# Moving two coefficient broadcasts behind the second half's loads at the start of an attention and two-network kernel

## The chip, the cores and the metric

One Trainium2 chip, of which the kernel uses one core. The metric is the device time of one execution in microseconds (us), as the median of several runs; less is better.

The engines are named as the profile names them: PE does the matmuls, DVE and ACT the elementwise work, POOL a part of it, and SP issues the transfers (DMAs). An engine takes its instructions strictly in the order in which the built program lists them, so an instruction that waits holds up everything behind it on its engine.

## The reference

Three stages follow each other: a linear attention with a decaying state, over 4 batches, 8 heads, 768 steps and head size 48; a network with a rational activation (384 to 2048 to 384); and a network with a softmax-like activation and a normalisation (384 to 1024 to 384), both over 3072 tokens.

```python
for t in range(S):                       # attention
    state = alpha[:, :, t, :, None] * state + np.einsum('bhd,bhe->bhde', k[:, :, t], v[:, :, t])
    y[:, :, t] = np.einsum('bhd,bhde->bhe', q[:, :, t], state)
...
h = x @ w_in                             # first network
P = a[0] + a[1] * h + a[2] * h2 + a[3] * h3
Q = 1.0 + np.abs(b[0]) * np.abs(h) + np.abs(b[1]) * h2
x = (P / (Q + 1e-06)) @ w_out
...
h = x @ w_in                             # second network
e = np.exp(h - h_max)
solu = h * e / (e.sum() + 1e-09)
out = ((solu - mu) / np.sqrt(var + 1e-06) * g_ln) @ w_out
```

The change concerns `a` (4 numbers) and `b` (2 numbers), the coefficients of the rational function.

## The kernel before

The 768 steps are cut into 6 chunks of 128 steps. A chunk of attention is done in two halves of two batches each, so that there are halves 0 to 11. The first network runs over 6 chunks of 16 blocks (`m_up` and `m_down`), while the halves of the chunks ahead are worked in between; the second network follows. The weights arrive as raw 64-bit data: `split_w` loads a tile (L533), makes a 32-bit float of it by three DVE instructions (L537, L540, L541), rounds it on ACT (L547) and takes the rest on POOL (L548).

The start of the program is the function `network(True)` from L806 on. Half 0 loads `alpha`, `k` and `q` (`a_load(0)`, L266, four transfers each), one weight tile, and `v` (`v_load(0)`, L348, two transfers). Then stands `consts()`: two small transfers that copy `a` and `b` into all 128 partitions (L113 into `ab`, L114 into `bb`), four tiny ACT instructions (L115, L117 to L119), a memset (L125) and 19 tiny DVE instructions (L120 to L139) that work out the coefficients `co`. Their first user is the first block of the first network (L599). After `consts()` come one more weight tile, `a_load(1)` and `v_load(1)` for half 1. PE transposes what half 0 and half 1 loaded (L363), DVE runs the decays over it (the scans of L374 and L378, the end values of L375 and L376, the products of L382 and L383), and `a_pe` does the matmuls of a half (L420, L444, L483) with an evacuation on ACT (L427) and on ACT and DVE (L470, L471).

The order on the engines is not the order of the source: the framework's scheduler lists each engine's instructions by a simulated timeline, in which the source order decides among what is ready. All these transfers go through SP's queue. The framework gives SP's transfers eight semaphores in turn, so that a transfer is issued only when the one eight places ahead of it has landed.

Names in the rows: `lent` is one of two borrowed buffers, of which one takes half 1's `alpha`, `k` and `q` (printed as `lent_128`) and the other a weight tile and half 1's `v` (`lent_175` before, `lent_149` after the change; the number is only a counter). `st` is the other place for a raw weight tile, `vns` half 0's `v`, `tp` a transposed tile, `qks` and `kns` half 0's operands.

Of the kernel before, what the change touches and what calls it, by code (L numbers as in the profile page):

```python
# [19 lines left out]
def _view(ap, off, dims):  # L20
    return bass.AP(ap.tensor, ap.offset + off, [list(ap.ap[0])] + [list(d) for d in dims])


def _run(*gens):
    for g in gens:
        for _ in g:
            pass
# [3 lines left out]
def kernel(  # L31
# [78 lines left out]
    def consts():  # L110


        nc.sync.dma_start(out=ab, in_=bass.AP(moe_a.tensor, moe_a.offset, [[0, 128], [1, 4]]))  # L113
        nc.sync.dma_start(out=bb, in_=bass.AP(moe_b.tensor, moe_b.offset, [[0, 128], [1, 2]]))  # L114
        nc.scalar.activation(babs, bb, AF.Abs)  # L115
        cf, lin, rc, beta, rest, t, base = (co[:, 2 * x:2 * x + 2] for x in range(7))
        nc.scalar.activation(cf[:, 0:1], bb[:, 1:2], AF.Abs)  # L117
        nc.scalar.activation(cf[:, 1:2], ab[:, 3:4], AF.Abs)
        nc.scalar.activation(lin[:, 0:1], bb[:, 0:1], AF.Abs)  # L119
        nc.vector.tensor_scalar(sign, ab[:, 3:4], 0.0, 2.0, ALU.is_ge, ALU.mult)  # L120
        nc.vector.tensor_scalar(sign, sign, 1.0, None, ALU.subtract)
        nc.vector.tensor_tensor(lin[:, 1:2], ab[:, 2:3], sign, ALU.mult)
        nc.vector.tensor_tensor(base[:, 1:2], ab[:, 1:2], sign, ALU.mult)
        nc.vector.tensor_tensor(a0s, ab[:, 0:1], sign, ALU.mult)
        nc.vector.memset(base[:, 0:1], QC)  # L125
        nc.vector.tensor_scalar(bad[:, 4 * NCH:4 * NCH + 2], cf, C_MIN, None, ALU.is_lt)
        nc.vector.tensor_scalar(cf, cf, C_MIN, None, ALU.max)
        nc.vector.reciprocal(rc, cf)
        nc.vector.scalar_tensor_tensor(beta, lin, 0.5, rc, ALU.mult, ALU.mult)
        nc.vector.tensor_tensor(t, beta, beta, ALU.mult)  # L130
        nc.vector.tensor_tensor(t, t, cf, ALU.mult)
        nc.vector.tensor_scalar(bad[:, 4 * NCH + 2:], t, BETA * BETA, None, ALU.is_gt)
        nc.vector.tensor_scalar(beta, beta, B_MAX, -B_MAX, ALU.min, ALU.max)
        nc.vector.tensor_tensor(t, beta, beta, ALU.mult)
        nc.vector.tensor_tensor(base, base, rc, ALU.mult)
        nc.vector.tensor_tensor(rest, base, t, ALU.subtract)
        nc.vector.tensor_tensor(a0s, a0s, rc[:, 1:2], ALU.mult)
        nc.vector.tensor_tensor(back, cf[:, 1:2], rc[:, 0:1], ALU.mult)
        nc.vector.tensor_tensor(back, back, sign, ALU.mult)  # L139
# [13 lines left out]
    def network(fast):  # L153
# [30 lines left out]
        def clear():  # L184
            nc.gpsimd.memset(d1, 0.0)
            nc.gpsimd.memset(_view(d1[:], 0, [[PER, NB6 + 1]]), 1.0)
            nc.gpsimd.memset(d2, 0.0)
            nc.vector.memset(alT[:, 0:1], 0.0)
# [3 lines left out]
        def borrow(n, o, dims):  # L192
            if n not in lent:
                lent[n] = moe_pool.tile([128, GW], F32, name=f"lent{n}", tag=f"g{n}")
            size = 1
            for d in dims:
                size *= d
            t = lent[n][:, o:o + size]
            if len(dims) == 1:
                return t  # L200
            nm = "abcd"[:len(dims)]
            return t.rearrange(f"p ({' '.join(nm)}) -> p {' '.join(nm)}", **dict(zip(nm, dims)))
# [44 lines left out]
        def slot(i, x):  # L247

            c, bp = divmod(i, 2)
            return c, 2 * bp + x // 2, 4 * (x % 2)  # L250

        def a_load(i, names=("ra", "rk", "rq")):
            for x, (src, nm) in enumerate(((alpha, "ra"), (k, "rk"), (q, "rq"))):
                if nm not in names:
                    continue
                if i == 1:
                    t = borrow(3, 2048 + 1024 * x, [16 * D + 16])
                elif i == 0 and nm == "rq":
                    t = borrow(3, 5120, [16 * D + 16])
                else:  # L260
                    t = ap_.tile([128, 16 * D + 16], F32, name=nm, tag="rk" if nm == "rk" else "ra")
                if i < NPE:
                    nc.gpsimd.memset(t[:, 16 * D:], 1.0)
                for y in range(B):
                    c, b, h = slot(i, y)
                    nc.sync.dma_start(  # L266
                        out=t[32 * y:32 * y + 32, :16 * D].rearrange("p (h x) -> p h x", h=4),
                        in_=src[b, h:h + 4, CH * c:CH * c + CH, :].rearrange("h (j r) d -> j h (r d)", r=4),
                    )
                raws[i, nm] = t  # L270
                yield

        def a_move_qk(i):
            qk, kb = moved[i]
            for m, i0, n, d0 in ((0, 0, 32, 0), (1, 0, 16, 32), (1, 16, 16, 64), (2, 0, 32, 80)):
                nc.sync.dma_start(out=qks[d0:d0 + n], in_=qk[m].rearrange("b i x -> i b x")[i0:i0 + n])
            yield
# [64 lines left out]
        def v_load(i):  # L342
            vn = vts[i] = borrow(2, 1024, [B * 256]) if i == 1 else vns
            if i < NPE:
                nc.vector.memset(_view(vn[:], D, [[64, 4 * B], [1, 16]]), 0.0)
            for x in range(2):
                c, b, h = slot(i, 2 * x)
                nc.sync.dma_start(  # L348
                    out=vn[:, 512 * x:512 * x + 512].rearrange("p (h d) -> p h d", h=H)[:, :, :D],
                    in_=v[b, :, CH * c:CH * c + CH, :].rearrange("h t d -> t h d"),  # L350
                )
# [48 lines left out]
        def a_prep(i):  # L400
            if i >= NPE:
                yield from a_dve(i)

        def a_enter(i):
            if i < NPE:
                v_load(i)
                yield from a_turn(i)
            else:
                yield from a_move(i)
# [142 lines left out]
        def w1_group(n):  # L552
            w = moe_pool.tile([128, GW], F32R, name=f"g{n}", tag=f"g{n}")
            hi, lo = (w[:, 512 * KT * x:512 * KT * (x + 1)].rearrange("p (a b) -> p a b", a=KT) for x in range(2))
            for kt in range(KT):
                split_w(moe_w_in[128 * kt:128 * kt + 128, 512 * n:512 * n + 512], hi[:, kt, :], lo[:, kt, :])
                yield
            wi[n] = (hi, lo)
            hi, lo = (w[:, 4 * DM * x:4 * DM * (x + 1)].rearrange("p (a b) -> p a b", a=4) for x in range(2, 4))
            for f in range(4):  # L560
                r0 = 512 * n + 128 * f
                split_w(moe_w_out[r0:r0 + 128, :], hi[:, f, :], lo[:, f, :])
                yield
            wo[n] = (hi, lo)
# [9 lines left out]
        def x_load(c):  # L574
            for kt in range(KT):
                nc.sync.dma_start(
                    out=x_tile(c)[:, kt].rearrange("p a t -> p (a t)").bitcast(F32), in_=y_d[c][128 * kt:128 * kt + 128, :]
                )
# [217 lines left out]
        def take(g, n):  # L796
            for _ in range(n):
                if next(g, "end") == "end":
                    return False
            return True  # L800
# [5 lines left out]
        if fast:  # L806
            stage["wide"] = True
            stage["bank"] = "x2"
            pre = w1_group(0)
            _run(a_load(0))  # L810
            take(pre, PRE[0])
            v_load(0)
            consts()
            take(pre, PRE[1])
            _run(a_load(1))
            take(pre, PRE[2])
            v_load(1)
            take(pre, PRE[3])
            nc.gpsimd.memset(Sbd, 0.0)
            _run(a_turn(0), a_pe(0), a_turn(1), a_pe(1), pre)  # L820
            clear()
            pre = w1_group(1)
            take(pre, NA)
            _run(a_load(2, ("ra", "rk")))
            with tc.issue_after(marks[0, 1].ins):
                _run(a_prep(2))
            _run(a_move_qk(2))
            _run(a_enter(2), pre)
            _run(a_load(3, ("ra", "rk")))
            stage["wide"] = False  # L830
            stage["near"] = True
            stage["bank"] = "at"
        else:
            for n in range(NG):
                _run(w1_group(n))
            x_load(0)
# [190 lines left out]
    with tc.If(wide > 0):  # L1027
        recurrence()
        network(False)
# [30 lines left out]
```

## Time and profile before

| | |
|---|---|
| median of 3 runs | 778.04 us (775.98 to 781.6) |
| the profiled execution's own time | 776.87 us |
| its span in the profile | 775.0 us |
| PE busy | 728.0 us (94% of the span) |
| DVE busy | 630.4 us (81%) |
| ACT busy | 535.2 us (69%) |
| POOL busy | 358.4 us (46%) |

The profiled execution's own time is 1.9 us more than its span. It lies 1.2 us under the median. Each share is an average over the whole span; the stretches below have different limits. In a row of the timeline the first number is the start and the second the length in us from the span's start, and the bracket gives the idle time of that engine just before and what ended it.

### The profile page before, as it was taken

Reading aid. Unit: us, or ns where it says so; the run is one execution under the profiler, and the core shown is the slowest. Engines: PE = TensorE matmul, PEld = TensorE weight load, DVE = VectorE, ACT = ScalarE, POOL = GpSimd, SP = SyncE. Lnnn points to the kernel's source line nnn. Section 1 sums busy time; section 2 is a strip of 40 time slices with the busy share of each in tenths; the row PEclk is TensorE's granted clock in tenths of the full one; section 3 lists DMA queues with packets and bytes.
Section 4 is the critical chain, followed back from the end, with each engine's and each line's share of the span. In section 5 each row is a group of like instructions: output and inputs, shape, how many; then the busy total and the mean of one; then the engine's idle time right before and its main releaser. Section 6 shows DMA issues by size and latency. Waiting matters only on the chain.

```text
span 775.0 us, 13914 instructions
## 1 busy us (share of the span) xinstructions
PE 728.0 (94%) x4976; PEld 605.8 (78%) x4976; DVE 630.4 (81%) x1110; ACT 535.2 (69%) x983; POOL 358.4 (46%) x306
## 2 busy tenths in 40 slices
PE   4676999999999999999999999999999999999996
PEld 3565767788888787778877788888888989988986
DVE  4999999989898989899898966478887788877640
ACT  2245867689878888788878887788965545555541
POOL 3255777777554355434444433332243343452322
PEclk9857899999999999999999999999999999999999
DMA  7995446466837382727554350720025253542653
GB/s 167 253 275 165 107 155 167 146 147 206 204 99 161 122 205 83 172 66 207 137 148 91 124 82 1 296 112 0 1 83 132 89 130 90 132 108 52 140 119 76
DMA packets 87278, 101.74 MB, mean 131 GB/s; under 512 B 34464, under 2 KB 63136, under 8 KB 87200
## 3 DMA queue, kind: packets, MB, share of 16 engines
q1 hardware_dynamic: 87104, 100.67, 48.9%
q8 instruction: 41, 0.67, 0.4%
q14 instruction: 37, 0.30, 0.1%
q10 hardware_dynamic: 96, 0.10, 0.0%
HBM read 60.59 MB, written 27.56 MB: 114 GB/s over the span
## 4 chain that ended last, share of the span: by engine, by line
DVE 30%; PE 18%; ACT 12%; issue 5%; SPq 3%; DMA 3%; POOL 1%; ACTq 0%; DVEq 0%; POOLq 0%
PE x2p L638 6%; PE hp L592 6%; DVE room L752 3%; SPq L762 3%; DVE room L735 2%; DVE p L618 2%; ACT jk L737 2%; PE op L776 2%; DVE hp L622 2%; DVE w L621 2%; DMA room<-room 2%; DVE sm L731 2%; DVE room L750 2%; PE h L712 2%; DVE p L623 2%
## 5 line engine op out<-in xcount | busy, mean ns | idle before, releaser
L592 PE MATMUL hp<-xt,g 128*128 128x512 f32 x864 | 224.1, 401 | 14.8 <-DVE p L616 7.5
L626 POOL TENSOR_TENSOR gl<-p,gh 128x512 fp32r<-128x512 f32 x96 | 130.8, 1362 | 193.9 <-ACT gh L625 107.9
L592 PEld LDWEIGHTS hp<-xt,g 128*128 128x128 f32 x864 | 163.2, 192 | 54.2 <-DVE p L616 7.7
L638 PE MATMUL x2p<-gh,g 128*128 128x512 f32 x576 | 196.9, 395 | 2.0 <-ACT x2e L646 2.0
L638 PEld LDWEIGHTS x2p<-gh,g 128*128 128x128 f32 x576 | 107.9, 188 | 29.1 <-ACT x2e L646 4.7
L638 PE MATMUL x2p<-gl,g 128*128 128x512 f32 x288 | 112.9, 392 | 0.0
L776 PE MATMUL op<-w2oh,room 128*128 128x384 f32 x384 | 101.8, 339 | 1.3 <-ACT room L767 0.7
L768 POOL TENSOR_TENSOR room<-room,room 128x1024 fp32r<-128x1024 f32 x22 | 54.8, 2496 | 101.0 <-ACT room L767 79.0
L621 DVE SCALAR_TENSOR_TENSOR w<-w,co,hp 128x512 f32<-128x512 f32 x84 | 62.0, 738 | 43.5 <-ACT hp L620 42.5
L712 PE MATMUL h<-w2ih,x 128*128 128x512 f32 x288 | 90.7, 394 | 0.0
L599 ACT ACTIVATE p<-hp,co 128x512 f32<-128x512 f32 x96 | 66.0, 687 | 12.3 <-POOL gl L626 12.0
L620 ACT ACTIVATE hp<-ah 128x512 f32<-128x512 f32 x84 | 50.1, 597 | 33.3 <-DVE p L618 32.0
L776 PEld LDWEIGHTS op<-w2oh,room 128*128 128x128 f32 x384 | 70.1, 188 | 3.0 <-ACT room L767 1.0
L600 ACT ACTIVATE w<-ah,co 128x512 f32<-128x512 f32 x96 | 69.4, 724 | 1.7 <-DVE hp L622 1.3
L618 DVE SCALAR_TENSOR_TENSOR p<-p,co,hp 128x512 f32<-128x512 f32 x84 | 61.6, 734 | 9.3 <-ACT p L599 9.0
L597 ACT ACTIVATE ah<-hp 128x512 f32<-128x512 f32 x96 | 56.7, 591 | 16.4 <-PE hp L592 16.0
L776 PE MATMUL op<-w2ol,room 128*128 128x384 f32 x192 | 65.0, 339 | 0.0
L625 ACT ACTIVATE gh<-p 128x512 fp32r<-128x512 f32 x96 | 59.9, 623 | 5.7 <-DVE p L623 2.8
L638 PEld LDWEIGHTS x2p<-gl,g 128*128 128x128 f32 x288 | 54.1, 188 | 11.7 <-issue 0.8
L712 PEld LDWEIGHTS h<-w2ih,x 128*128 128x128 f32 x288 | 53.9, 188 | 11.7
L623 DVE SCALAR_TENSOR_TENSOR p<-p,co,hp 128x512 f32<-128x512 f32 x84 | 61.9, 737 | 1.1
L619 ACT ACTIVATE ah<-w,co 128x512 f32<-128x512 f32 x84 | 60.6, 721 | 1.3
(168 smaller groups left out, 1264.7 us busy)
## 6 DMA issues: line engine op xcount, KB each, us to landing
room<-room SPq DMA_DIRECT2D x96, 128.0 KB, 2.3
qk_d<-qk SPq DMA_DIRECT2D x10, 771.0 KB, 4.1
st<-in_moe_w_in_dram SPq DMA_DIRECT2D x13, 512.0 KB, 4.6
st<-in_moe_w_out_dram SPq DMA_DIRECT2D x16, 384.0 KB, 3.5
qks<-qk_d SPq DMA_DIRECT2D x20, 257.0 KB, 4.4
x<-x_d SPq DMA_DIRECT2D x18, 256.0 KB, 3.1
out_dram<-o SPq DMA_DIRECT2D x94, 48.0 KB, 1.6
ra<-in_alpha_dram SPq DMA_DIRECT2D x44, 96.0 KB, 2.8
```

Of the source, the lines that this page charges most:

```text
L592: last["PE", u] = nc.tensor.matmul(hp, lhsT=w[:, kt, 128 * o:128 * o + 128], rhs=xts[c][:, kt, xx, :], start=(kt == 0 and w is hi and xx = ...
L599: nc.scalar.activation(p, hp, AF.Square, bias=co[:, 7:8])
L600: nc.scalar.activation(w, ah, AF.Square, bias=co[:, 6:7])
L618: nc.vector.scalar_tensor_tensor(p, p, a1, hp, ALU.add, ALU.mult)
L619: nc.scalar.activation(ah, w, AF.Ln, bias=rest)
L621: nc.vector.scalar_tensor_tensor(w, w, rest, hp, ALU.add, ALU.mult)
L623: fin[u] = nc.vector.scalar_tensor_tensor(p, p, a0, hp, ALU.add, ALU.mult)
L625: last["ACT", u] = nc.scalar.activation(gh, p, AF.Copy)
L626: last["POOL", u] = nc.gpsimd.tensor_tensor(gl, p, gh[:].bitcast(F32), ALU.subtract)
L638: nc.tensor.matmul(x2ps[c][d], lhsT=w[:, o, 128 * d:128 * d + 128], rhs=gg, start=(f == 0 and w is hi and gg is gh), stop=(f == NF1 - 1 an ...
L712: nc.tensor.matmul(hp[:, 512 * n:512 * n + 512], lhsT=x2s[c][:, kt, x, CH * b:CH * b + CH], rhs=w2[w][:, kt, 512 * n:512 * n + 512], start ...
L776: nc.tensor.matmul(op, lhsT=x[:, 128 * f:128 * f + 128], rhs=w2[w][:, f, :], start=(f == 0 and x is hi and w == "oh"), stop=(f == NF2 - 1 ...
```

## The change

The call of `consts()` moves from behind `v_load(0)` to behind `v_load(1)`. Nothing else in the source changes.

```diff
             v_load(0)
-            consts()
             take(pre, PRE[1])
             _run(a_load(1))
             take(pre, PRE[2])
             v_load(1)
+            consts()
             take(pre, PRE[3])
```

On SP, behind the load of half 0's `v`, the built program before has:

```order
L348 DMA vns<-in_v_dram 128x8x48 x2
L113 DMA ab<-in_moe_a_dram 128x4
L114 DMA bb<-in_moe_b_dram 128x2
L533 DMA lent_175<-in_moe_w_in_dram 128x512
L266 DMA lent_128<-in_alpha_dram 32x4x192 x4
L266 DMA lent_128<-in_k_dram 32x4x192 x4
L266 DMA lent_128<-in_q_dram 32x4x192 x4
L348 DMA lent_175<-in_v_dram 128x8x48 x2
L533 DMA st<-in_moe_w_in_dram 128x512
```

and after the change:

```order
L348 DMA vns<-in_v_dram 128x8x48 x2
L533 DMA lent_149<-in_moe_w_in_dram 128x512
L266 DMA lent_128<-in_alpha_dram 32x4x192 x4
L266 DMA lent_128<-in_k_dram 32x4x192 x4
L266 DMA lent_128<-in_q_dram 32x4x192 x4
L348 DMA lent_149<-in_v_dram 128x8x48 x2
L113 DMA ab<-in_moe_a_dram 128x4
L114 DMA bb<-in_moe_b_dram 128x2
L533 DMA st<-in_moe_w_in_dram 128x512
```

The two broadcasts moved past one weight tile and 14 loads of half 1; the weight tile into `st` is next behind them now.

On DVE, behind the second scan of half 0 (L374), before:

```order
L540 SCALAR_TENSOR_TENSOR fp<-st,fp 128x512
L120 TENSOR_SCALAR co<-ab 128x1
L375 TENSOR_SCALAR qks<-Pp 128x4
L126 TENSOR_SCALAR bad<-co 128x2
L541 SCALAR_TENSOR_TENSOR ft<-st,fp 128x512
L121 TENSOR_SCALAR co<-co 128x1
L376 RECIPROCAL Rp<-qks 128x4
L127 TENSOR_SCALAR co<-co 128x2
L383 TENSOR_TENSOR qks<-tp,Pp 128x4x128
L537 TENSOR_SCALAR fp<-lent_175 128x512
```

and after, from the same place:

```order
L540 SCALAR_TENSOR_TENSOR fp<-st,fp 128x512
L375 TENSOR_SCALAR qks<-Pp 128x4
L541 SCALAR_TENSOR_TENSOR ft<-st,fp 128x512
L376 RECIPROCAL Rp<-qks 128x4
L383 TENSOR_TENSOR qks<-tp,Pp 128x4x128
L537 TENSOR_SCALAR fp<-lent_149 128x512
L378 SCALAR_TENSOR_TENSOR Rp<-tp,Rp,zero 128x127 x4
L540 SCALAR_TENSOR_TENSOR fp<-lent_149,fp 128x512
L382 TENSOR_TENSOR qks<-tp,Rp 128x4x128
L374 SCALAR_TENSOR_TENSOR Pp<-tp,zero 128x128 x4
L541 SCALAR_TENSOR_TENSOR ft<-lent_149,fp 128x512
```

The reader of `ab` (L120) and the first reader of what ACT makes of `bb` (L126) no longer stand in front of L541. They stand further down now, inside half 1's first pair of head groups, among the scans of L378:

```order
L375 TENSOR_SCALAR end_392<-Pp 128x4
L376 RECIPROCAL Rp<-end_392 128x4
L378 SCALAR_TENSOR_TENSOR Rp<-tp,Rp,zero 128x127 x3
L120 TENSOR_SCALAR co<-ab 128x1
L378 SCALAR_TENSOR_TENSOR Rp<-tp,Rp,zero 128x127
L121 TENSOR_SCALAR co<-co 128x1
L126 TENSOR_SCALAR bad<-co 128x2
L382 TENSOR_TENSOR lent_128<-tp,Rp 128x4x128
```

Beyond that the scheduler gave other orders on all engines up to the end of the first network's first chunk (about 185 us in the trace); behind that the lists of the path that runs are equal.

## Rows read from the trace of the kernel before

**Rows 1.** Stretches: length, busy time (count) of each engine, granted clock, DMA share, GB/s.
```profile
13.00:20.00 7.00, 1.15 (x18) 0.96 (x16) 3.32 (x14) 2.48 (x9) 2.63 (x4) 0.85 0.79 173
20.00:60.00 40.00, 29.46 (x323) 24.76 (x323) 39.07 (x95) 13.98 (x30) 15.51 (x16) 0.71 0.95 263
60.00:150.00 90.00, 77.94 (x542) 61.33 (x546) 88.65 (x148) 64.74 (x118) 68.65 (x58) 0.91 0.52 144
150.00:185.00 35.00, 35.00 (x248) 28.53 (x240) 31.58 (x51) 29.69 (x55) 24.82 (x22) 1.00 0.60 155
```

**Rows 2.** Timeline of DVE, 13 to 30 us.
```profile
13.25 0.67 DVE L540 SCALAR_TENSOR_TENSOR fp<-st,fp 128x512 int32<-128x512 int32 x1
...
16.02 0.17 DVE L126 TENSOR_SCALAR bad<-co 128x2 f32<-128x2 f32 x1 [1.97 <-ACT co L117]
...
16.89 0.68 DVE L383 TENSOR_TENSOR qks<-tp,Pp 128x512 f32<-128x512 f32 x1
19.29 0.69 DVE L537 TENSOR_SCALAR fp<-lent 128x512 int32<-128x512 int32 x1 [1.71 <-DMA lent<-in_moe_w_in_dram]
...
20.17 1.58 DVE L378 TENSOR_TENSOR_SCAN Rp<-tp,Rp,zero 128x127 f32<-128x127 f32 x4
...
22.32 0.15 DVE L135 TENSOR_TENSOR co<-co 128x2 f32<-128x2 f32 x1
22.39 0.15 DVE L137 TENSOR_TENSOR co<-co 128x1 f32<-128x1 f32 x1
...
29.49 0.67 DVE L383 TENSOR_TENSOR lent<-tp,Pp 128x512 f32<-128x512 f32 x1
```

**Rows 3.** Timeline of SP's issues, 6 to 23 us.
```profile
6.92 1.06 SPq L348 DMA_DIRECT2D vns<-in_v_dram  x2
8.03 2.82 SPq L113 DMA_DIRECT2D ab<-in_moe_a_dram  x1
10.88 0.43 SPq L114 DMA_DIRECT2D bb<-in_moe_b_dram  x1
11.36 0.44 SPq L533 DMA_DIRECT2D lent<-in_moe_w_in_dram  x1
11.84 1.85 SPq L266 DMA_DIRECT2D lent<-in_alpha_dram  x4
13.74 5.85 SPq L266 DMA_DIRECT2D lent<-in_k_dram  x4
...
21.53 1.16 SPq L348 DMA_DIRECT2D lent<-in_v_dram  x2
22.74 0.65 SPq L533 DMA_DIRECT2D st<-in_moe_w_in_dram  x1
```

**Rows 4.** Half microseconds of the same view as rows 1.
```profile
12.00:12.50 0.50, 0.50 (x14) 0.50 (x12) 0.50 (x3) 0.00 (x0) 0.00 (x0) 1.00 0.18 20
...
13.00:13.50 0.50, 0.50 (x10) 0.50 (x10) 0.50 (x3) 0.20 (x1) 0.00 (x0) 1.00 0.03 1
13.50:14.00 0.50, 0.50 (x12) 0.46 (x10) 0.50 (x3) 0.00 (x0) 0.00 (x0) 1.00 0.75 91
```

**Rows 5.** DMA issues of 8 to 12 us: count, KB each, us to landing.
```profile
lent<-in_moe_w_in_dram SPq DMA_DIRECT2D x1, 512.0 KB, 7.9
...
ab<-in_moe_a_dram SPq DMA_DIRECT2D x1, 2.0 KB, 5.0
bb<-in_moe_b_dram SPq DMA_DIRECT2D x1, 1.0 KB, 4.8
```

**Rows 6.** DMA issues of 22 to 23 us, the second of half 1's v loads among them.
```profile
st<-in_moe_w_in_dram SPq DMA_DIRECT2D x1, 512.0 KB, 5.3
lent<-in_v_dram SPq DMA_DIRECT2D x1, 192.0 KB, 4.0
```

**Rows 7.** SP's issue behind two v loads later in the kernel.
```profile
159.30 2.96 SPq L282 DMA_DIRECT2D kns<-kb_d  x1
```

**Rows 8.** Longest wait of DVE from 60 to 185 us: total, times, longest.
```profile
DVE hp L610 <- ACT p L599: 2.7, 4, 1.7
```

## Prediction

> **What bounds the kernel now.** The page's busy shares name PE (94%), but as an average. I therefore read the stretches first [rows 1]: from 20 to 150 us DVE is busy for 39.07 of 40 and 88.65 of 90 us, while PE has 29.46 and 77.94. Up to 150 us DVE sets the pace, and it is idle for only 0.93 + 1.35 = 2.28 us in all that time. From 150 to 185 us PE is busy for 35.00 of 35 us and takes over. So a microsecond that DVE wins or loses in the first 20 to 30 us is carried along by DVE to 150 us and then by PE. Behind about 185 us the lists of both programs are equal.
>
> The place of the change is the hole before that: from 13 to 20 us DVE has only 3.32 of 7 us, so it idles for 3.68 us [rows 1]. Its timeline shows why [rows 2]. L126 waits for 1.97 us until ACT has made coefficients of `bb`, and then L537 waits for 1.71 us on the weight tile in `lent`. Both are transfers, so SP's timeline comes next [rows 3]. Behind the two `v` loads the broadcast of `ab` takes 2.82 us to issue, where `bb` takes 0.43, and the weight tile comes only at 11.36 us, half 1's `alpha` at 11.84. Last the half microseconds of the DMA [rows 4]: from 12.0 to 13.5 us it moves 20, then 1 GB/s. Here only the broadcasts are under way, and the weight tile, issued by 11.80 us, brings data only from about 13.5 us on.
>
> **The change, part by part.** No work is added or taken away: two transfers, 4 ACT and 19 tiny DVE instructions and a memset are the same before and after. What can change is idle time of DVE and the order.
>
> First the loads that come forward. The weight tile takes `ab`'s place behind the `v` loads. I take the 2.82 us for the price of that place, not of `ab`: `bb`, of the same kind, took 0.43 [rows 3], and another transfer behind two `v` loads took 2.96 us [rows 7]. So the tile's issue ends at 8.03 + 2.82 = 10.85 us instead of 11.80, which is 0.95 us earlier, and `alpha`'s loads likewise come forward by 0.96 us. That is the lower bound. The upper bound is that the hole is closed whole: data from 12.0 us on instead of from 13.5 to 14.0, up to 1.9 us [rows 4]. I take 1.4 us, about the middle. DVE then gets the tile at 19.29 - 1.4 = 17.9 us.
>
> The row shows that the tile's data starts only when the broadcasts' packets are nearly through [rows 4]. The Trainium skill ("DMA: Bandwidth & Descriptors", section "Queues, rings and completion order") says that on each DMA engine descriptors are consumed in ring order. By that rule the tile would win the whole 1.9 us; by the issue alone 0.95.
>
> Then DVE's way to the tile. Its L540 ends at 13.92 us [rows 2]. Before, the stretch from L126's start at 16.02 to L383's end at 16.89 + 0.68 = 17.57 us took 1.5 us. Now L541 to L383 follow L540 at once and end at 15.4 us, and DVE waits there until 17.9. The wait on `bb` is gone from here, but the one on the tile is 2.5 us instead of 1.71: so far the win is the 1.4 us of the tile, not the 1.97 us of L126.
>
> Then the broadcasts in their new place. Between the tile and L120 stand four passes over 512 columns, 11 scans and two tiny instructions: 4 x 0.68 + 11 x 1.58/4 + 0.2 = 7.3 us [rows 2], of which some is overlap; I take 7.0, so DVE comes to L120 at 24.9 us. SP: before, the last of the four `k` loads had to wait for the tile (issued at 11.36, landed 7.9 us later, at 19.26 [rows 5]; the group of `k` issues ends at 13.74 + 5.85 = 19.59 [rows 3]). The order of eight semaphores is the same after, so `q` and `v` shift with the tile: `v` at 20.1 to 21.3 us, `ab` at 21.35, and, at 0.43 to 0.65 us each, `bb` at 21.9 and the tile into `st` at about 22.4 instead of 22.74. `ab` can't land before the second `v` load in front of it, which landed 4.0 us after its issue at 22.0 [rows 6], so 24.6 us now; at `bb`'s 4.4 us behind its issue's end it would be 26.2. I take 25.4. `bb` lands 4.8 us behind its issue [rows 5]: 26.7. ACT then needs 0.3 us (before: `bb` landed at 10.88 + 4.8 = 15.7, L126 began at 16.02), so L126 can begin at 27.0 us. DVE waits 0.5 us at L120, runs its last scan (0.4) and waits about 1.1 us at L126, with everything behind it on DVE held up: L382 and L383 of half 1, and the splits of the next weight tiles.
>
> The sum. From L126 at 27.0 us there remain, up to the point that the kernel before reaches at 29.49 + 0.67 = 30.16 us, three passes (L382, L383, L537: 2.0 us) and 17 tiny instructions at 22.39 - 22.32 = 0.07 us each (1.2 us): 27.0 + 2.0 + 1.2 = 30.2 us. **That is a shift of 0.0 us**: the 1.4 us won at the tile is given back at L120 and L126, because the 3 KB of broadcasts pass through the same queue later and DVE asks for them about as soon as they can be there. The tile into `st`, landed 5.3 us behind its issue [rows 6], is there at 27.7 to 28.1 us, before L537 asks for it at about 28.4.
>
> ACT's four instructions wait for the same broadcasts and hold up one evacuation (L427) behind them; it is off DVE's path as long as it isn't later than before. PE's clock is 0.85 of full in 13 to 20 us and 0.71 in 20 to 60 [rows 1], between the levels of 2.4 and 1.2 GHz; PE stays ahead of DVE there in either case, so I cost it at nothing.
>
> The other orders up to 185 us I cannot derive. From above they can win no more than the 2.28 us that DVE idles. For a loss the nearest row is DVE's longest wait between 60 and 185 us, 1.7 us [rows 8]. I take zero.
>
> Against its own time the profiled execution gives 776.87 + 0.0 = 776.9 us; the median of the runs is 778.04, 1.2 us above it. I forecast 777.5 us, between the two: **no change**.
>
> **Rivals.** *The broadcasts come in time.* If `bb` has landed when DVE reaches L126, and the hole is closed whole (the tile at 17.4 us), DVE gets there at 24.4 + 0.5 = 24.9 us instead of 27.0. That is 2.1 us faster: 774.8 us. For it speaks that the hole lies in front of the tile alone; against it, that `bb` needed 4.8 us to land behind a nearly empty queue, and is asked for 3 us after its issue. The whole hole of 3.68 us is the bound.
>
> *The stall behind the v loads moves with the broadcasts.* Slower: `ab` is now the transfer behind half 1's two `v` loads. If it pays 2.96 us as in rows 7, its issue ends at 24.3 us, `bb` lands at 24.3 + 4.8 = 29.1 and L126 begins at 29.4 instead of 27.0: 2.4 us later, 779.3 us; with the tile only 0.95 us earlier, 2.9 us. It decides as soon as `ab` takes over 0.4 us longer than the 0.65 us that the transfer at this place took before (22.74 us [rows 3]). That 0.65 speaks against it, the 2.82 and 2.96 for it. The Trainium skill, on the same page under "Rules for kernel authors", advises to issue a transfer early and to wait for it late; the change issues these two late and asks for them soon. By that rule the outcome is this rival's. The trace of before bears it out so far as DVE's one wait for them, 1.97 us, stood in a hole that DVE had anyway.
>
> *The new order costs more.* DVE and PE have other lists from 30 to 185 us. A wait of 1.7 us [rows 8] once or twice gives up to 781 us; five of them would be needed for 1%.
>
> **How the numbers follow.** No change (within 1.5 us): 0.55. Broadcasts in time: 0.18. Stall behind `v`: 0.18. New order, mostly slower: 0.09. The low end is the whole hole, 776.87 - 3.68 = 773.2, rounded to 773.0; the high end is the median with the stall's 2.9 us and one wait of 1.7, 778.04 + 4.6 = 782.6, rounded to 782.5. One per cent, 7.8 us, is about what a measurement of this kernel tells from no change. Faster by it would need more than the 3.68 + 2.28 = 5.96 us that DVE idles from 13 to 150 us: 0.03. Slower by it needs several waits together: 0.05. That leaves 0.92 for the same.
>
> **What would show it.** In the changed profile: DVE's L537 at 17.4 to 18.4 us behind a wait of 2 to 3 us (right), or at 19.3 as before (the hole was not the broadcasts'). The tile's issue at 8.03 with about 2.8 us (the place's price), or 0.43 (then `ab`'s own). L120 and L126 with waits of about 0.5 and 1.1 us; none would mean the fast rival, over 3 us the slow one. L383 of half 1 ending near 29.6 and the state of 30.2 us reached at 30 to 31 us. From 30 to 150 us DVE still idle for about 2 us. If DVE shows several us of new waits there, the order was the cause and the forecast is wrong.

## The result, and the profile after

| | median | runs |
|---|---|---|
| kernel before | 778.39 us (774.28 to 781.6) | 20 |
| changed kernel | 782.77 us (777.76 to 784.82) | 20 |

The ratio is 1.0052, with a 95% interval of 1.0033 to 1.0071: 4.4 us slower. That is less than the one per cent that the prediction took for the least that can be told from no change, but with 20 runs of each kernel the interval is only 0.2% to either side, so the loss is there. The median lies 0.3 us above the forecast range. In 12 further runs beside 35 of the kernel before it was 782.21 against 777.44, a ratio of 1.0055 (1.003 to 1.008).

One thing has to be known to read the profiles: the four profiled executions of the changed kernel took 777.6 to 778.8 us, while 20 of its 30 other runs took 782 to 785, so the profiles show only about half of the loss.

First the stretches of the changed kernel (length, busy time and count of PE, PE's weight loads, DVE, ACT and POOL, granted clock, DMA share, GB/s), with one of ten microseconds added:

```profile
13.00:20.00 7.00, 3.19 (x39) 2.94 (x37) 6.04 (x15) 2.54 (x6) 2.64 (x4) 0.86 0.85 220
20.00:60.00 40.00, 27.18 (x308) 22.32 (x304) 36.70 (x94) 14.30 (x34) 15.29 (x17) 0.71 0.87 250
60.00:150.00 90.00, 75.36 (x497) 59.37 (x498) 87.34 (x143) 63.56 (x116) 62.33 (x56) 0.89 0.52 140
150.00:185.00 35.00, 35.00 (x275) 28.04 (x274) 32.17 (x52) 29.32 (x54) 25.61 (x23) 1.00 0.60 155
130.00:140.00 10.00, 5.79 (x29) 4.25 (x28) 9.91 (x16) 6.42 (x14) 9.06 (x8) 0.71 0.42 115
```

The last of these in the kernel before:

```profile
130.00:140.00 10.00, 8.74 (x44) 6.73 (x42) 9.90 (x20) 6.60 (x14) 9.70 (x10) 1.00 0.45 139
```

Against [rows 1], the hole of DVE is nearly gone: 6.04 of 7 us busy in 13 to 20, where it had 3.32. From 20 to 150 us, however, DVE now idles for 3.30 + 2.66 = 5.96 us in place of 2.28, all but 0.2 us of it before 90 us. From 130 to 140 us DVE is as busy as before, and PE does 5.79 us of work in place of 8.74, at a granted clock of 0.71 in place of full speed.

SP's issues, to be held against [rows 3]:

```profile
8.03 3.37 SPq L533 DMA_DIRECT2D lent<-in_moe_w_in_dram  x1
11.45 1.86 SPq L266 DMA_DIRECT2D lent<-in_alpha_dram  x4
...
18.68 1.06 SPq L348 DMA_DIRECT2D lent<-in_v_dram  x2
19.79 0.96 SPq L113 DMA_DIRECT2D ab<-in_moe_a_dram  x1
20.79 0.43 SPq L114 DMA_DIRECT2D bb<-in_moe_b_dram  x1
```

The long issue stayed in its place behind half 0's `v` loads, and the weight tile pays it now. Behind half 1's `v`, `ab` takes 0.96 us. Then the landings (issues of 8 to 12.5 us, and below the dots of 19.5 to 22 us; the last number is us from the issue's start to the landing):

```profile
lent<-in_moe_w_in_dram SPq DMA_DIRECT2D x1, 512.0 KB, 7.9
...
ab<-in_moe_a_dram SPq DMA_DIRECT2D x1, 2.0 KB, 3.5
bb<-in_moe_b_dram SPq DMA_DIRECT2D x1, 1.0 KB, 4.6
```

The tile lands 7.9 us behind the start of its issue, as before [rows 5], although 3.37 us of that are now the issue itself. The two equal numbers are chance: over all profiles it is 5.5 to 7.9 us with the broadcasts ahead (7 profiles) and 6.7 to 8.3 with the broadcasts behind (12). Half microseconds of the DMA, as in [rows 4]:

```profile
12.00:12.50 0.50, 0.50 (x14) 0.50 (x12) 0.50 (x2) 0.00 (x0) 0.00 (x0) 1.00 0.92 213
13.00:13.50 0.50, 0.50 (x10) 0.41 (x8) 0.50 (x3) 0.00 (x0) 0.00 (x0) 1.00 0.99 262
22.00:22.50 0.50, 0.50 (x13) 0.50 (x12) 0.36 (x4) 0.45 (x1) 0.00 (x0) 1.00 0.23 20
23.00:23.50 0.50, 0.50 (x14) 0.50 (x12) 0.50 (x2) 0.50 (x2) 0.50 (x1) 1.00 0.44 17
```

The hole at 12.0 to 13.5 us is filled, and one like it stands at 22 to 24 us, where the broadcasts are now. Last DVE's timeline, to be held against [rows 2]:

```profile
16.00 0.69 DVE L537 TENSOR_SCALAR fp<-lent 128x512 int32<-128x512 int32 x1 [0.34 <-DMA lent<-in_moe_w_in_dram]
...
23.56 0.13 DVE L120 TENSOR_SCALAR co<-ab 128x1 f32<-128x1 f32 x1
...
25.77 0.17 DVE L126 TENSOR_SCALAR bad<-co 128x2 f32<-128x2 f32 x1 [1.65 <-ACT co L117]
...
27.16 0.68 DVE L383 TENSOR_TENSOR lent<-tp,Pp 128x512 f32<-128x512 f32 x1
27.76 0.68 DVE L537 TENSOR_SCALAR fp<-st 128x512 int32<-128x512 int32 x1
```

DVE has the tile at 16.00 us, 3.3 us earlier, and waits 1.65 us for `bb` at L126. At 28.44 us its three passes are done, and 12 of the 17 tiny instructions are left, 0.8 us at 0.07: it stands where the kernel before stands at 30.16 about 0.9 us earlier. So the start won. Then DVE waits for ACT before the first block of the first network, 2.2 us in place of 0.5 us (the view of waits, 60 to 185 us, of the changed kernel and, below the dots, of the kernel before):

```profile
DVE fp L537 <- ACT lent L396: 2.2, 1, 2.2
...
DVE fp L537 <- ACT lent L396: 0.5, 1, 0.5
```

All profiles agree on this. With the broadcasts behind (12 profiles) DVE is ready for this L537 at 66.1 us in the mean, with the broadcasts ahead (7) at 67.8, 1.7 us later; but it then waits 1.1 to 2.2 us in the 12 and 0.4 to 0.8 in the 7. What it waits for is ACT's copy of PE's last transposes (L396 behind L392), and PE in the changed kernel works from 60.18 to 68.29 us without a pause, up to 66 us at a granted clock of 0.5. So about 1 us of the win stays there, and the first L597 comes at 68.0 us in place of 68.5 (means; single profiles lie between 65.9 and 70.0).

The loss that the profiles show is in the stretch from the first block (its first ACT instruction, L597) to the 17th. The changed kernel:

```profile
69.24 0.60 ACT L597 ACTIVATE ah<-hp 128x512 f32<-128x512 f32 x1 [0.42 <-PE hp L592]
...
164.20 0.60 ACT L597 ACTIVATE ah<-hp 128x512 f32<-128x512 f32 x1 [0.17 <-PE hp L592]
```

and the kernel before:

```profile
69.07 0.60 ACT L597 ACTIVATE ah<-hp 128x512 f32<-128x512 f32 x1 [0.42 <-PE hp L592]
...
162.30 0.60 ACT L597 ACTIVATE ah<-hp 128x512 f32<-128x512 f32 x1 [0.19 <-PE hp L592]
```

94.96 us in place of 93.23. The largest difference in PE's waits in it is at 133 us. On DVE of the changed kernel:

```profile
133.04 2.41 DVE L308 TENSOR_TENSOR_SCAN P<-alT,d 128x774 f32<-128x774 f32 x1
135.37 1.12 DVE L540 SCALAR_TENSOR_TENSOR ft<-st,ft 128x384 int32<-128x384 int32 x1
136.41 0.75 DVE L615 SCALAR_TENSOR_TENSOR hp<-hp,co,ah 128x512 f32<-128x512 f32 x1
137.07 0.73 DVE L623 SCALAR_TENSOR_TENSOR p<-p,co,hp 128x512 f32<-128x512 f32 x1
```

In the kernel before this scan stood ahead of L610 and L622:

```profile
128.19 1.76 DVE L308 TENSOR_TENSOR_SCAN P<-alT,d 128x774 f32<-128x774 f32 x1
...
134.11 0.90 DVE L540 SCALAR_TENSOR_TENSOR ft<-st,ft 128x384 int32<-128x384 int32 x1
134.94 0.73 DVE L623 SCALAR_TENSOR_TENSOR p<-p,co,hp 128x512 f32<-128x512 f32 x1
```

PE waits for L623, 3.19 us now and, below the dots, 1.23 before:

```profile
137.86 3.77 PE L592 MATMUL hp<-xt,g 128*128 128x512 f32 x9 [3.19 <-DVE p L623]
...
135.73 2.35 PE L592 MATMUL hp<-xt,g 128*128 128x512 f32 x9 [1.23 <-DVE p L623]
```

### The profile page after: what moved, and what is told of

Its sections match the earlier page's. It is cut to its first block, busy times and chain, and to the rows that moved or that the text cites. A ratio compares the mean times of both kernels' runs of the same rounds, so it can differ in the third digit from the quotient of the medians.

```text
span 777.1 us, 13916 instructions
## 1 busy us (share of the span) xinstructions
PE 727.7 (94%) x4976; PEld 604.7 (78%) x4976; DVE 631.5 (81%) x1110; ACT 536.2 (69%) x983; POOL 354.2 (46%) x306
## 4 chain that ended last, share of the span: by engine, by line
DVE 36%; PE 26%; ACT 12%; DMA 10%; SPq 7%; issue 6%; POOL 2%; DVEq 0%; ACTq 0%; POOLq 0%
PE hp L592 11%; PE x2p L638 10%; SPq L762 4%; DVE room L752 3%; DVE hp L622 3%; DVE p L618 2%; DVE room L735 2%; DVE w L621 2%; DMA rq<-in_q_dram 2%; ACT jk L737 2%; DVE sm L731 2%; SPq L266 2%; DVE p L623 2%; DVE P L308 2%; DVE room L750 2%
## 5 line engine op out<-in xcount | busy, mean ns | idle before, releaser
L768 POOL TENSOR_TENSOR room<-room,room 128x1024 fp32r<-128x1024 f32 x22 | 54.8, 2495 | 101.0 <-ACT room L767 93.9
L599 ACT ACTIVATE p<-hp,co 128x512 f32<-128x512 f32 x96 | 65.9, 686 | 10.5 <-POOL gl L626 10.1
L597 ACT ACTIVATE ah<-hp 128x512 f32<-128x512 f32 x96 | 56.6, 590 | 16.8 <-PE hp L592 16.6
L623 DVE SCALAR_TENSOR_TENSOR p<-p,co,hp 128x512 f32<-128x512 f32 x84 | 61.9, 737 | 1.1
```

Of the source, the lines that this page charges most:

```text
L599: nc.scalar.activation(p, hp, AF.Square, bias=co[:, 7:8])
L623: fin[u] = nc.vector.scalar_tensor_tensor(p, p, a0, hp, ALU.add, ALU.mult)
```

## The experiments

**Four kernels on order and place.** The prediction could not derive the scheduler's other orders and took zero for them, so here they were held fixed. At the end of the path that runs, each engine's instructions are chained by issue order without any wait, in the order of one kernel or the other:

```diff
-        moe.__exit__(None, None, None)
+        moe.__exit__(None, None, None); fast and _force(tc, RUNS)
```

`RUNS` lists the rows of the two kernels' orders. They are cut where the same instructions lie ahead on both sides (row 329 of PE, 182 of DVE, 68 of ACT, 54 of POOL, 58 of SP), at about 91 us; SP runs ahead and is cut at about 49. What is called the head below is thus the place of the broadcasts together with all that the scheduler ordered otherwise up to there. The first kernel of the four has no such list; it is the changed kernel.

> The changed kernel once more, the same order of instructions on every engine. Its 20 times lay in two groups, 6 at 777.8 to 780.5 us and 14 at 782.0 to 784.8, and its profile (778.8 us) shows only the first. Expected: the median again at 782 to 783, a ratio of 1.003 to 1.007. If the profile falls into the upper group, the theory (DVE's new order around 130 us, where TensorE's granted clock fell to 0.71 for ten microseconds) expects its extra 4 us between 125 and 180 us too, and the milestones after 200 us shifted by a constant; the rival (a clock that falls by chance later on) expects them behind 200 us.

> The kernel before with its own order of instructions up to the row that runs at about 91 us, and from there on, on all five engines, the order of the changed kernel: its two broadcasts stand ahead of the second half's loads, as before, and only the later order is new. Theory (the new order around 130 us costs the time): 780.5 to 782.8 us against 778.4, 2 to 4.4 us slower. Rival (the broadcasts' new place costs it through the first 91 us): 778.4, no difference.

> The other half: the changed kernel's own order up to about 91 us, the broadcasts behind the second half's loads, and from there on the order of the kernel before on all five engines. Theory (later order): 777.4 to 778.6 us, no slower than the kernel before, since both stand within 0.2 us of each other at 69 us. Rival (head): 780.5 to 782.8.

The fourth undoes six rows of DVE in the changed kernel:

```diff
+L308 SCALAR_TENSOR_TENSOR P<-alT,d_109 128x774
+L610 SCALAR_TENSOR_TENSOR hp<-p,co,hp 128x512
 L537 TENSOR_SCALAR ft<-st 128x384
-L610 SCALAR_TENSOR_TENSOR hp<-p,co,hp 128x512
+L622 SCALAR_TENSOR_TENSOR hp<-w,hp 128x512
 L493 TENSOR_TENSOR Sbd<-Sbd,u 48x8x48 x2
-L622 SCALAR_TENSOR_TENSOR hp<-w,hp 128x512
-L308 SCALAR_TENSOR_TENSOR P<-alT,d_109 128x774
```

> The changed kernel with one thing undone: six DVE instructions that run at 128 to 134 us stand as in the kernel before, the scan of L308 ahead of L610, L537, L622 and the two L493 in place of behind them. Theory in its narrow form (that scan, 2.4 us, stands ahead of L615 and L623 and makes TensorE wait): most of the loss is gone, 778.5 to 780.5 us. If the loss comes from several places of the new order, or from the head, it stays at 781.5 to 783.

| kernel | median, 12 runs | ratio to before (777.44), interval |
|---|---|---|
| changed kernel again | 782.21 us | 1.0055, 1.003 to 1.008 |
| old head, new order | 781.16 us | 1.0032, 1.0009 to 1.0054 |
| new head, old order | 775.93 us | 0.998, 0.9958 to 1.0002 |
| new, scan early | 778.32 us | 1.0008, 0.9989 to 1.0027 |

The loss belongs to the order behind 91 us: with the old head it costs 3.7 us, and taken from the changed kernel it leaves 1.5 us less than before, more than either expectation gave, with an interval that just reaches no difference. Six rows are worth 3.9 us of it. As to the source line, the arithmetic was no part: a program with only the two transfers at the old place and the arithmetic at the new one, built but not run, has, but for two memsets, the order of the kernel before on every engine.

The granted clock is not what tells these kernels apart. Its median over the whole run is 0.969 in the 35 runs of the kernel before and 0.965 in the changed kernel's 32, but 0.964 in the kernel with the scan early, which is 3.9 us faster.

**The six rows the other way, the broadcasts left out, and two more profiles.** The kernel without broadcasts:

```diff
-        nc.sync.dma_start(out=ab, in_=...)
-        nc.sync.dma_start(out=bb, in_=...)
+        nc.vector.memset(ab, 0.5)
+        nc.vector.memset(bb, 0.5)
```

> The kernel before, broadcasts ahead of the second half's loads and all its order kept, but for the six DVE instructions at 128 to 134 us: the scan of L308 stands behind L610, L537, the two L493 and L622, as in the changed kernel. Theory (these six instructions cost the time, whatever the head): 780.5 to 782.0 us, 3 to 4.5 slower than the kernel before, since undoing them in the changed kernel brought it from 782.2 to 778.3. Rival (they cost only together with the changed head, whose phase they meet): 777.4 to 778.5.

> The kernel before with all its order kept and the two coefficient broadcasts left out: ab and bb are filled with 0.5 by two memsets on VectorE, so the network is computed with other coefficients. It bounds what any place of the broadcasts can give. Theory (the new place gains 1.0 to 1.5 us by 30 us, since the second w_in tile is issued and lands earlier; SP's stall of 2.8 us stays with whatever stands behind the v loads): L537 gets that tile at 15.5 to 16.5 us in place of 19.3, SP's issue behind the v loads still takes 2.5 to 3.4, time 775 to 777 us. Rival (the head is hidden by the half-clock chain before 69 us, and the 1.5 us of the earlier run were chance): 777.4 to 778.5.

> The changed kernel, one look for a profile. 20 of 32 of its times lie at 782 to 785 us, and both profiles so far (778.8 and 777.6) are of the others. If this one is above 782, theory: TensorE's wait for block 9's L623 and the lower granted clock behind it stand between 125 and 185 us and last longer than in the two lower profiles (block 24's L597 at 206 to 209 us in place of 203 to 205). Rival: the extra time lies before 69 us or behind 200.

> The changed kernel, a second look for a profile, with the same expectations: above 782 us the extra time stands between 125 and 185 us by the theory, elsewhere by the rival; below 781 the milestones of the two lower profiles come again.

The scan late in the kernel before: 778.93 us against 777.94, ratio 1.0012 (0.9987 to 1.0037). That is between the two expectations and nearer the rival's. So the six rows cost little or nothing there, and the theory's first form, that they cost by themselves, fell. Without broadcasts: 776.63 us, ratio 0.9987 (0.9969 to 1.0005), in the theory's range, though no difference is not excluded. Its SP's issue behind half 0's `v` loads:

```profile
8.03 3.08 SPq L533 DMA_DIRECT2D lent<-in_moe_w_in_dram  x1
```

and its DVE at the weight tile:

```profile
15.87 0.69 DVE L537 TENSOR_SCALAR fp<-lent 128x512 int32<-128x512 int32 x1 [0.32 <-DMA lent<-in_moe_w_in_dram]
```

The place's stall is there with no broadcast in the program, and the tile comes at 15.87 us, as in the changed kernel: the new place wins at the tile all that could be won. The two further profiles took 778.8 and 778.3 us, so the question that they were taken for stays unanswered: none of the four profiles is of a run above 782. If a profiled run were like any other, that would be a chance of about one in eighty (a third, four times).

**Cut kernels: where the time is lost in the runs that are timed.** Since the profiles do not show it all, both kernels, each with its own order, were cut off at four places and timed.

```diff
-        for u in range(NU + LAG):
+        for u in range(20 if fast else NU + LAG):
```

> The kernel before, cut off: its main loop ends behind 20 of its 100 steps, the first network's first 512 tokens, and everything behind that (the rest of both networks and the output) is left out; the order of what is left is that of the kernel before up to about 190 us. It is the measure for the two runs beside it: 188 to 200 us, by the trace of before, in which the step 20 begins at 183.6 us.

> The changed kernel cut off at the same place, everything behind 20 of the main loop's 100 steps left out, its own order kept up to about 190 us. Theory (the time is lost between 91 and 185 us by the new order): 4 to 5 us slower than the cut kernel before, as the whole kernels' medians differ by 4.9. Rival (only the 2 us that the profiles show are lost there, and 2 to 3 more arise behind 185 us, where the clock or the second network stand otherwise): 1.5 to 2.5 slower.

> The changed kernel cut off at the same place (all behind 20 of 100 steps left out), with the six DVE instructions at 128 to 134 us as in the kernel before. Theory: within 1 us of the cut kernel before, 3.5 to 4.5 below the cut changed one, as in the whole kernels. Rival (what the scan's place costs arises behind 185 us): within 1 us of the cut changed kernel.

> The kernel before cut off behind 80 of the main loop's 100 steps: the first network's last 512 tokens and the second network are left out; order as before. The measure for the run beside it: 503 to 512 us, by the trace of before, where block 80 begins at 492.5 us.

> The changed kernel cut off behind 80 of 100 steps (the last 512 tokens of the first network and the second network left out). The kernels cut behind 20 steps differ by 0.8 us, the whole ones by 4.9. If the other 4 us arise in steps 20 to 79: 4 to 5 us slower than the cut kernel before. If they arise behind step 80, in the last steps or in the second network: 0.5 to 1.5 slower.

> The kernel before with the whole main loop, the first network and the second network's first four tiles, and without tiles 4 to 23 and the output. The measure for the run beside it: 598 to 612 us, by the trace of before, where the first eviction L785 behind the loop stands at 605.5 us.

> The changed kernel with the whole main loop, without tiles 4 to 23 of the second network and the output. If the 4 us arise in the loop's steps 80 to 99, while the second network's weights are loaded: 4 to 5 slower than the cut kernel before, with 0.5 to 1.5 for the kernels cut behind 80. If they arise in the last stage alone, which this kernel leaves out: 0.5 to 1.5 slower here too, and the last stage has a slower course that the changed kernel falls into more often, as one profile has shown it (the kernel without broadcasts: 206.0 us from the last L597 to the end, 202.0 to 202.7 in nine other profiles).

> The kernel before with the second network's last stage cut off behind its tile 13 (tiles 14 to 23 and most of the output are left out). The measure for the run beside it: 660 to 680 us, by the trace of before, where the L731 of that tile stands at 654 us.

> The changed kernel cut off behind tile 13 of the last stage (tiles 14 to 23 and most of the output are left out). The kernels cut before that stage differ by 1.7 us, the whole ones by 4.9. Theory: the rest comes in tiles 4 to 13, where DVE's instructions of 128x1 stand 2.1 us each behind POOL's L768 and a third such hit (as in the profile of the kernel without broadcasts, 62 to 71 us behind the last L597) is decided by 0.1 us: 3.5 to 5 slower than the cut kernel before. Rival: it comes behind tile 13, at the end: 1 to 2.5 slower.

| cut | old (5 or 6 runs) | new | difference |
|---|---|---|---|
| 20 of 100 steps | 197.24 us | 198.02 us | 0.8 us |
| the same, new with scan early | | 197.93 us | 0.7 us |
| 80 steps | 499.31 us | 501.92 us | 2.6 us |
| whole main loop | 603.81 us | 605.52 us | 1.7 us |
| behind tile 13 | 672.27 us | 674.30 us | 2.0 us |
| whole (35 runs old, 12 new) | 777.44 us | 782.21 us | 4.8 us |

With so few runs, of one kernel up to 5 us apart, a difference here is good to 1 us at 20 steps and for the whole loop, and to about 2 us at 80 steps and behind tile 13. The old kernel cut behind 80 steps stood 3.7 us below its expected range, the other three in theirs. So the theory, 4 to 5 us lost before step 20, fell, and so did 4 to 5 us by the end of the main loop. About 2 us are lost by there. Behind tile 13 the difference is in the rival's range, but the theory's 3.5 us are only unlikely. The other 2 to 3 us show in none of the cut programs. The scan's place, worth 3.9 us in the whole kernel, is worth 0.1 when the kernel is cut behind 20 steps, so what it is worth does not arise where it stands.

**All profiles together.** 20 profiles of full and cut kernels hold the stretch up to block 17, and those that run so far from there to block 96 (L597, from the 1st to the 17th and from the 17th to the 96th):

| order behind 91 us | 1st to 17th L597 | 17th to 96th |
|---|---|---|
| old (8 profiles) | 92.6 to 93.4 us, one 95.8 | 404.2 to 404.4 us |
| new (9) | 94.0 to 96.1 us, mean 94.9 | 404.6 to 404.8 us |
| new, scan early (2) | 95.9 and 96.2 us | 404.7 us |
| old, scan late (1) | 92.6 us | 404.3 us |

The one at 95.8 is the first profile of the new head with the old order, in which DVE waits 2.4 us for a weight tile in this stretch (1.0 in the second). Without it the old order's mean is 93.1, with it 93.4: the new order costs 1.9 us (1.5 with it) up to block 17 and 0.4 behind, together the 2 us of the cut kernels. The old head with the new order shows it too:

```profile
65.90 0.59 ACT L597 ACTIVATE ah<-hp 128x512 f32<-128x512 f32 x1
...
161.08 0.60 ACT L597 ACTIVATE ah<-hp 128x512 f32<-128x512 f32 x1 [0.17 <-issue]
```

That is 95.18 us. With the scan early the stretch is not shorter, so the wait of PE at 134 us was a symptom, and with it the lower granted clock behind it, which these two have as well (0.84 and 0.70 from 130 to 140 us). DVE is full and loses the time elsewhere. Part of where: I summed, in that stretch, by how much DVE instructions exceeded the lower quartile of their kind (same operation, same shapes), where it was over 0.25 us. That is 5.8 to 6.7 us in the old order, mean 6.4, and 6.9 to 8.6 us in the new, mean 7.7: about 1.3 of the 1.9 us are the same instructions taking longer. Each of these 10 to 14 instructions of a profile began while an instruction of POOL was running, and one of POOL ended during it. The pair at 133 us shows how. POOL of the changed kernel ran

```profile
132.56 1.26 POOL L614 TENSOR_TENSOR w<-w,ah 128x512 f32<-128x512 f32 x1
133.90 2.18 POOL L494 TENSOR_TENSOR Sbd<-Sbd,end 48x384 f32<-48x384 f32 x1
```

and L308 and L540, each begun while POOL worked, took 2.41 and 1.12 us, where the kernel before has 1.76 us for that scan and 0.90 for that L540, which POOL held there too (0.54 is its length at 139.19 us).

**The kernel that came out ahead, again.**

> The changed head with the order of the kernel before from 91 us on, once more, since it stood below the kernel before (775.9 against 777.4) with an interval that just reached no difference. If the new place of the broadcasts gains by itself: 775.5 to 777.0, a ratio below 0.999. If not: 777 to 778.5.

775.15 us against 777.98, ratio 0.9974 (0.9951 to 0.9997). The new head with the order of before beats both kernels, if by 0.3% only, and by a little more than was expected. Its DVE at the weight tile, in the profile of this run:

```profile
16.32 0.69 DVE L537 TENSOR_SCALAR fp<-lent 128x512 int32<-128x512 int32 x1 [0.37 <-DMA lent<-in_moe_w_in_dram]
```

and its first and 17th L597:

```profile
68.02 0.60 ACT L597 ACTIVATE ah<-hp 128x512 f32<-128x512 f32 x1 [0.42 <-PE hp L592]
...
161.39 0.60 ACT L597 ACTIVATE ah<-hp 128x512 f32<-128x512 f32 x1 [0.36 <-PE hp L592]
```

The tile comes 3 us earlier than in the profile of the kernel before, about as in the changed one, and the stretch of 16 blocks is 93.37 us long, as the old order has it.

## Why the prediction was wrong, point by point

- **What bounds the kernel: right from 90 us on, wrong before.** From 90 to 150 us DVE is busy for 59.5 of 60 us in the kernel before and 59.8 in the changed one, and in the profiles what is lost there stays lost to block 96. But a microsecond won at the start is not carried along whole. I cost PE and its clock at nothing, since PE stays ahead of DVE up to 60 us, and let DVE set the pace to 150; at 66 us PE is not ahead. DVE, ready 1.7 us earlier there in the mean, waits 1 us longer for what comes from PE.
- **The 2.82 us are the price of the place: right.** The weight tile paid 3.37 us there, 3.08 with no broadcast in the program, and `ab` 0.96 and `bb` 0.43 in the new place.
- **The tile 1.4 us earlier: wrong in size.** It came 3.3 us earlier, beyond both bounds (0.95 and 1.9); over all profiles it landed at 15.7 us in place of 18.6, 2.9 earlier (means of 12 and 7). I priced only the start of its data. By the trace's record of packets (the tile is 128 of 4096 bytes) the first began at 12.03 us in place of 13.64, 1.6 us earlier and within my bounds. But in the old place the data then took longer as well: 4.5 us to the end of the last packet, with the packets of `bb` under way up to 15.15 us, in place of 3.3, and 1.1 us from there to the landing in place of 0.6. I had put that at no change. The rule of the Trainium skill ("DMA: Bandwidth & Descriptors", section "Queues, rings and completion order") that I weighed here, descriptors consumed in ring order, fits the first packet (1.9 us by it, 1.6 measured) better than the 0.95 by the issue's end; neither has the longer transfer.
- **Waits of 0.5 and 1.1 us at L120 and L126: right in sum, by two shifts that cancel.** None and 1.65 us. DVE came to L120 at 23.56 in place of 24.9 us, and `bb` landed at 20.79 + 4.6 = 25.4 in place of 26.7, since SP's last `k` load waits for the tile, as I had it, and the tile came earlier than I had it.
- **A shift of 0.0 at 30 us: wrong by about 0.9 us**, because the tile came earlier than I had it and let SP issue the broadcasts earlier: L126 began at 25.77 us in place of 27.0. With the order behind 91 us held, the new head is worth 1.5 and 2.8 us in two sets of 12 runs; the first interval reaches no difference, the second (0.2 to 3.8 us) does not. How much of that is the broadcasts' place and how much the other order up to 91 us, no run tells apart.
- **The other orders at zero: this step failed, and it decided the sign.** The new order costs 3.7 us with the old head and 6.3 with the new one (782.21 less 775.93). My bound for a loss, one wait of 1.7 us, looked at waits, as I had said that only idle time of DVE and the order can change. The lengths of DVE's instructions change too: those beside POOL are no waits in that view, and about 1.3 of the 1.9 us that the profiles show are of this kind.
- **The rivals.** "The new order costs more" came true in its sign, not by its mechanism of one or two waits; it had 0.09. The stall did not move with the broadcasts (0.96 us for `ab`, 0.31 over the 0.65 where 0.4 were needed). "In time" did not come: L126 waits as forecast.
- **Open.** The other 2 to 3 us are in the times of whole kernels only, and six rows of DVE at 130 us switch them off without shortening their own stretch. Neither the profiles nor the cut kernels show where they arise. Behind tile 13, or in the whole program only, is what the runs favour.

## What to carry to other kernels

Where a scheduler sorts the instructions, an edit is two edits: the one in the source, and the new order that comes with it. Price them apart by holding the order fixed: here the move, with the order up to 91 us, won 1.5 to 2.8 us and the order behind lost more. A time read from one pair of profiles can be chance too: the tile's 7.9 us to landing in both kernels was. And for an effect of half a per cent, compare many times before one profile, since the executions that were profiled here were not the typical ones.

## What the runs showed of the hardware that was not expected

The stall behind half 0's `v` loads has one end in all 20 profiles. Whatever stood there, the broadcast of `ab` or the weight tile, its issue took 2.28 to 3.87 us and ended 0.36 to 0.38 us after the last packet of the weight tile three places ahead (the one into `st`, issued at 6.45 us) had begun: at 10.85 and 10.47 us in the kernel before, at 11.41 and 11.04 in the changed one. The first packet of a tile issued in that place began 0.6 to 0.8 us behind the end of its issue, so no data of it moved while the issue stood. Why the issue waits for that tile, no run shows.

DVE can be held by POOL for as long as POOL's instruction lasts, and which of DVE's instructions meets it is a matter of 0.1 to 0.2 us. The kernel without broadcasts had the longest second network of eleven full profiles (206.0 us from the 96th L597 to the last L785; the others 201.2 to 202.7). Its DVE, tiny instructions first at their usual length:

```profile
620.72 0.16 DVE L748 SCALAR_TENSOR_TENSOR sm<-sm 128x1 f32<-128x1 f32 x1
...
621.11 0.81 DVE L750 TENSOR_SCALAR room<-room,sm 128x1024 f32<-128x1024 f32 x1
...
626.61 2.15 DVE L747 TENSOR_TENSOR sm<-sm 128x1 f32<-128x1 f32 x1 [2.24 <-ACT sm L746]
628.78 2.41 DVE L748 SCALAR_TENSOR_TENSOR sm<-sm 128x1 f32<-128x1 f32 x1
...
631.42 2.87 DVE L750 TENSOR_SCALAR room<-room,sm 128x1024 f32<-128x1024 f32 x1
```

and its POOL:

```profile
626.32 4.86 POOL L768 TENSOR_TENSOR room<-room,room 128x1024 fp32r<-128x1024 f32 x2 [19.11 <-ACT room L767]
631.35 2.38 POOL L768 TENSOR_TENSOR room<-room,room 128x1024 fp32r<-128x1024 f32 x1 [0.17 <-ACT room L767]
```

L747, usually 0.16 us, ends at 628.76 and L748 at 631.19, with the first two L768 (626.32 + 4.86 = 631.18); L750 begins 0.07 us behind the third and ends half a microsecond behind it. In the kernel before L750 began ahead of the third L768 and took its usual 0.81 us, and it is L768 that took longer, 2.93 us in place of 2.38:

```profile
635.81 0.81 DVE L750 TENSOR_SCALAR room<-room,sm 128x1024 f32<-128x1024 f32 x1
...
635.95 2.93 POOL L768 TENSOR_TENSOR room<-room,room 128x1024 fp32r<-128x1024 f32 x1 [0.19 <-ACT room L767]
```

That is one hit of 2.1 us on DVE fewer. The Trainium skill ("SBUF — State Buffer", section "Who interferes with whom") says that DVE and GpSimd (POOL) share a pair of ports, which a DVE instruction needs if it has two inputs in SBUF or runs in a two-port mode, and that the one that issues first has it for its whole instruction while the other is blocked. These rows agree: L747 and L748, of two inputs, end with POOL's instructions, and L750 and the third L768 change places. Whether such a hit makes the 2 to 3 us that stayed open, no run shows: the difference of 2.0 us between the kernels cut behind tile 13 speaks against this one, if weakly.
